# k'v of batches 1 to 7 as 64-column products, two heads side by side in the array

## The chip, the cores and the metric

The kernel runs on one core of one Trainium2 chip. A core has TensorE (the matrix array; the profile shows its products as PE and the loads of its weights as PEld), VectorE (DVE), ScalarE (ACT), GpSimd (POOL) and SyncE (SP), which issues most of the DMAs. The metric is device time in microseconds (us). Before the change it is 492.36 us, the median of three runs (492.21 to 492.42).

## The reference

Linear attention, and behind it a mixture of four experts over all tokens. There are 8 batches, 8 heads, 576 rows and 64 columns a head; 4608 tokens of 512 features; 4 experts with 1024 hidden units.

```python
def _attn_ref(q, k, v):
    phi = lambda x: np.where(x > 0, x, np.exp(x) - 1.0) + 1.0
    q_p, k_p = (phi(q), phi(k))
    kv = np.einsum('bhsd,bhse->bhde', k_p, v)
    z = np.sum(k_p, axis=2)
    num = np.einsum('bhsd,bhde->bhse', q_p, kv)
    den = np.einsum('bhsd,bhd->bhs', q_p, z)[..., None] + 1e-06
    return num / den

def _moe_ref(x, domain_probs, w1, w2):      # x: the attention's output, tokens by 512
    p = domain_probs / (domain_probs.sum(-1, keepdims=True) + 1e-09)
    for e in range(E):
        out += p[:, e:e + 1] * (np.maximum(x @ w1[e], 0.0) @ w2[e])
```

What the change touches is `kv` together with `z`: for each batch and head a matrix of 64 by 64, and the column sums of phi(k) as a 65th column. In the kernel v carries a constant column, so that both come from one product of k' (phi(k), 576 rows by 64) with v (576 rows by 65).

## The kernel before

**Staging.** A batch is one tile of 512 tokens (rows 0 to 511 of the batch, four to a partition) for the experts. The 64 rows that are left over of each batch are gathered into a ninth tile. The attention of batch b+1 is worked in between the expert products of tile b: while TensorE does the layers of tile j, the other engines load and prepare the next batch and TensorE does its small products at set places.

**Attention of a batch 1 to 7** (class `Batch`). `phi_act` (ACT, L343 and L346) and `phi_dve` (DVE, L351) make phi of k and q from the loaded data, the exponential passing through a PSUM bank of the pool "s"; `vcast` (ACT, L356) copies v to 16 bits. `left_act`, `left_v` and `left_dve` do the same for the 64 rows left over: `kl` holds their k' (with the other half of the partitions zero) and `vl` their v. `kv` makes the products of k' and v: for each pair of heads five products accumulate in PSUM, four over 128 rows each (L442) and one for the rows left over (L449). The stationary operand is k' of two heads, 128 columns, and the moving one v of two heads, 130 columns; so the result has four blocks of 64 by 65, of which the two on the diagonal are k'v of the two heads and the other two are not used. Two pairs go into one PSUM bank. Then ACT copies the diagonal blocks into `kvz` (L459), a tile whose other blocks stay zero, so that `nd` (L478) can multiply q' of two heads with it in one product of 130 columns and `norm` (L465, L466, DVE) can divide.

`kv` is called twice in a batch: `kv0` for pairs 0 and 1, `kv1` for pairs 2 and 3. Each call takes its own bank from the pool "s", which has two.

**Batch 0** (class `First`) is done before the experts start, with its rows laid out differently. Its `kv` (L612) already works by tiles: 64 rows and 64 columns of the array, the two halves on the array's diagonal.

**Experts.** For tile 0 the first layer of expert 0 (L661) and the second layer of all experts (L721) are plain products; all else goes by a Strassen-like scheme of seven products (`Block`, L873, for layer 1; `layer2_product`, L816, for layer 2), with its sums on POOL (`hidden_sum`, L783 to L789; `token_sum`, L854) and on DVE (L768 to L774 for the weights, L712 for the result, L857 for relu with an added part), and copies of banks on ACT (L884, L899, L906, L927).

**Order.** Nothing is left to a scheduler: each engine runs its instructions in the order in which the program issues them. All steps have a name and a due position (`CFG`, `put_at`) and are sorted by it; a step that is a generator stops at `yield` and goes on when its name comes again. The list `EARLY` writes out the order by hand for the first part, up to the first products of batch 3's turn; in it, a name that stands twice is the step's first part (for `kv` the products) and its second (the copies). In the later part a step's parts are issued directly one after the other. In a batch from 3 on, `kv0` is due at 17.5 and `kv1` at 19.1 of the batch's turn, with four products of layer 1, four of layer 2, four of layer 1 and four of layer 2 in between. In batch 1, two products of 512 columns stand between the two; in batch 2, two of 512 columns and eight of 256.

Of the kernel before, what the change touches and what calls it, by code (L numbers as in the profile page):

```python
# [11 lines left out]
FP32 = mybir.dt.float32  # L12
# [21 lines left out]
            lv=23.45,  # L34
            lk=15.35,
            lkd=16.3,
            kv=(33.6, 34.0),
            q=(36.4, 36.95, 40.2, 43.4),
            qd=(37.75, 39.0, 40.55, 44.7),
            lq=54.05,  # L40
# [13 lines left out]
            lv=10.36,  # L54
            lk=9.9,
            lkd=11.6,
            kv=(17.5, 19.1),
            q=(20.1, 22.1, 27.0, 30.0),
            qd=(21.75, 27.2, 30.2, 32.3),
            lq=33.9,  # L60
# [32 lines left out]
        "y0.33 k2 k0 y0.10 p1.020 p3.010 b1.k3 b1.lkm w211 p3.011 p1.021 y0.11 v3 s0.1 y0.20 w130 y0.12 y0.33 y0.13 p1.021 p2.021 p1.020 y0.21 y0.22 p2.020",  # L93
        "s2.0 s2.1 s2.3 b1.v1 p2.021 y0.13 p2.020 p6.020 p6.021 p6.020 t0.3 s2.2 y0.23 p6.021 b1.km3 p5.020 p7.020 b1.v2 q2 y0.23 s0.2 y1.10 t1.0 p7.020",
        "c22.020 b1.k1 p5.021 y1.11 p7.021 p7.021 w131 b1.km1 b1.k0 p4.020 p3.020 y1.20 y1.21 q0 b1.k2 p4.020 p4.021 c22.021 p3.020 b1.load5 p3.021 b1.km0",
        "y1.12 b1.v3 p4.021 b1.kv0 b1.km2 b1.load0 b1.kv0 y1.13 b1.kv1 b1.kv1 p3.021 y1.22 y1.23 b1.q3 y1.30 y1.13 y1.23 q1 y1.31 y1.32 y1.33 b1.q2 p1.031",
        "p1.031 y1.00 p1.030 p1.030 b1.qm3 y1.33 b1.qT3 b1.qm2 y1.01 b1.qT2 s3.0 s3.1 p2.030 y1.02 b1.qT3 b1.nd30 y1.03 s3.3 b1.qT2 b1.nd21 b1.loadlq p6.030",
        "b1.load2 lpr w220 p2.030 b1.nd30 w221 b1.q1 y1.03 p6.030 p5.030 b1.qm1 b1.nd31 p2.031 p7.030 b1.q0 b1.nd31 p6.031 b1.qm0 b1.next y2.00 p7.030 y2.01",
        "p4.030 p2.031 b1.qT1 p6.031 p4.030 b1.nd21 w230 b1.qT0 b1.nd20 p7.031 c22.030 p5.031 b1.qT0 b1.nd00 b1.xT3 s3.2 b1.nd20 b1.nd01 b1.qT1 p3.030 b1.xT2",
# [2 lines left out]
        "p1.100 p6.101 b1.qTl ts1.3 p3.031 b2.load0 y2.32 y2.33 b1.load3 t2.0 b2.lv p2.101 p6.100 p6.100 y2.33 b2.lkm y2.10 y2.11 t2.1 t0.1 b2.lq p2.100 p2.100",  # L102
        "y2.12 y2.13 b2.v0 p2.101 t3.0 b2.load5 p6.101 ts1.2 p7.100 y3.20 p7.100 b2.k3 y3.21 b2.v1 b2.load2 p5.100 p7.101 p7.101 b2.k1 b2.load3 y2.13 b1.nl",
        "y3.22 b2.km0 c22.100 b1.nl y3.23 b2.km3 y3.23 p3.100 p3.100 p4.100 b2.load9 p4.100 p5.101 b2.v2 b2.k2 b2.lqm y3.23 y3.10 y3.00 y3.01 p4.101 y3.02",
        "y3.03 p1.110 b2.km1 b2.kv0 p4.101 hs10.00 t1.1 b2.v3 y3.11 p1.110 p6.110 b2.kv0 c22.101 y3.03 b2.load4 b2.km2 p2.110 b2.kv1 p6.110 p2.110 y3.12 y3.13",
        "hs10.01 b2.q0 b2.kv1 p3.101 p7.110 t2.2 hs10.03 b2.load10 pr1 y3.30 p1.111 y3.31 b2.q1 p1.111 y3.32 t2.3 y3.33 y3.13 m10.21 p6.111 p5.110 hs10.02",
        "p3.101 b2.q3 b2.qm0 y3.03 b2.qm1 p7.110 p4.110 m10.20 y3.33 m10.21 hs10.10 t1.3 m10.51 b2.qm3 b2.q2 b2.load6 p2.111 m10.20 m10.50 hs10.11 m10.51",
        "p6.111 c22.110 b2.qm2 p4.110 b2.qTl p3.110 p3.110 m10.11 y3.13 m10.50 m10.11 p2.111 p7.111 p7.111 y3.33 b2.qT p1.120 m10.10 m10.61 p1.120 m10.10",
        "p2.120 p5.111 p2.120 m10.60 p6.120 m10.61 t0.2 t3.1 hs10.13 m10.31 m10.60 m10.30 c22.111 hs11.00 t1.2 p5.120 b2.load7 p4.111 b2.next m10.31 hs10.12",
# [13 lines left out]
def kernel(  # L123
# [10 lines left out]
    nc = tc.nc  # L134
# [6 lines left out]
    P = 128  # L141
    HP = P // 2
    CM = S // P
# [4 lines left out]
    NPAIR = H // 2  # L148
# [5 lines left out]
    DE = D + 1  # L154
# [54 lines left out]
    def aps(shape, dtype, name, more=""):  # L209
        return ppm.tile(shape, dtype, tag=CFG["BANK"].get(now[0] + more, "s"), bufs=2, name=name)  # L210
# [67 lines left out]
    class Batch:  # L278
# [153 lines left out]
                self.qT = pa.tile([P, CM, NPAIR, P], FP16, tag="qT", bufs=1, name="qT")  # L432
            (eng.copy if eng is nc.scalar else eng.tensor_copy)(out=self.qT[:, :, pair], in_=ps)

        def kv(self, pair0, n=2):
            ps = aps([P, 2, 2, DE], FP32, "psum_kv")
            for i in range(n):
                pair = pair0 + i
                hs = slice(2 * pair, 2 * pair + 2)
                a = pair % 2  # L440
                for c in range(CM):
                    nc.tensor.matmul(  # L442
                        out=ps[:, i],
                        lhsT=self.kp[:, c, hs],
                        rhs=self.vp[:, c, hs],
                        start=c == 0,
                        stop=False,
                    )
                nc.tensor.matmul(  # L449
                    out=ps[:, i],  # L450
                    lhsT=self.kl[:, pair],
                    rhs=self.vl[:, 2 * a : 2 * a + 2],
                    start=False,
                    stop=True,
                )
            yield
            for u in range(2):
                us = slice(u * HP, (u + 1) * HP)
                nc.scalar.copy(  # L459
                    out=self.kvz[us, pair0 : pair0 + n, u, :], in_=ps[us, 0:n, u, :]  # L460
                )

        def norm(self, dst, ps, n):
            recip = pa.tile([P, 4, 2, 1], FP32, tag="recip", bufs=3, name="recip")
# [470 lines left out]
    def order_of(at):  # L935

        return [x for _, x in sorted((at[n][i], (n, i)) for n in "vkq" for i in range(4))]

    def batch_steps(bt, nxt, put, at, at_next):

        mine = order_of(at)
        later = mine + (order_of(at_next) if nxt is not None else [])
        first = bt.b == 1

        def load(m):
            if m < len(later):
                (bt if m < len(mine) else nxt).load(*later[m])

        def load_left():
            if nxt is not None:  # L950
                nxt.alloc_left()
                nxt.load_left("k", "v", "q")

        b = bt.b

        def numerators(i0, n):
            yield from bt.nd(i0, n)
            for pair in range(NPAIR):
                if i0 < (pair + 1) * CM <= i0 + n:
                    yield  # L960
                    bt.dma_xT(pair)

        if not first:
            put(min(at["v"][0], at["k"][0], at["lv"], at["lk"]) - 0.01, f"b{b}.ones", bt.ones)
        for m, (n, i) in enumerate(mine):
            if n == "v":
                put(at[n][i], f"b{b}.v{i}", bt.vcast, i)
            else:
                put(at[n][i], f"b{b}.{n}{i}", bt.phi_act, n, i)
                put(at[n + "d"][i], f"b{b}.{n}m{i}", bt.phi_dve, n, i)  # L970
            if not first:
                put(at[n][i] + 1, f"b{b}.load{m}", load, m + NRAW)
        put(at["lv"], f"b{b}.lv", bt.left_v)
        for n in "kq":
            put(at["l" + n], f"b{b}.l{n}", bt.left_act, n)
            put(at["l" + n + "d"], f"b{b}.l{n}m", bt.left_dve, n)
        for i in range(2):
            put(at["kv"][i], f"b{b}.kv{i}", bt.kv, 2 * i)
        put(at["lqd"] + 1, f"b{b}.next", load_left)
        if not first:  # L980
            put(at["lqd"] + 2, f"b{b}.qTl", bt.dma_qTl)
        if first:
            put(at["qtl"], f"b{b}.qTl", bt.pe_qTl)
            for i in range(NPAIR):
                put(at["qt"][i], f"b{b}.qT{i}", bt.pe_qT, i, nc.scalar)
                for hf in range(2):
                    put(at["nd"][i], f"b{b}.nd{i}{hf}", bt.nd, i * CM + 2 * hf, 2)
                put(at["xt"][i], f"b{b}.xT{i}", bt.pe_xT, i)
            for i in range(NRAW):
                put(at["next"][i], f"b{b}.load{i}", load, len(mine) + i)  # L990
        else:
            put(at["qT"], f"b{b}.qT", bt.dma_qT)
            for i in range(6):
                put(at["nd"][i], f"b{b}.nd{i}", numerators, 3 * i, min(3, NPAIR * CM - 3 * i))
        put(at["nl"], f"b{b}.nl", bt.nd_left)
        if first:
            put(at["xl"], f"b{b}.xl", bt.pe_xl)
# [10 lines left out]
    b0, b1 = bts[0], bts[1]  # L1008
    on = {"A": nc.scalar, "V": nc.vector, "P": nc.gpsimd, "S": nc.sync}
    with tc.manual_schedule(  # L1010
# [7 lines left out]
        def put_at(pos, name, *g):  # L1018
            work.append((pos, len(work), name, g))
# [48 lines left out]
        for n, (j, e) in enumerate(units):  # L1068
            h, hss = [None, None], [[None] * 4, [None] * 4]
            at = base + 2 * NSLOT * n  # L1070
# [11 lines left out]
            if n == len(units) - 1:  # L1082
                order, at = (1, 2, 6, 5, 7, 3, 4), at + NSLOT
# [3 lines left out]
        for j in range(0, NTILES - 1):  # L1087
            at = base + 2 * NSLOT * E * (j - 1) if j else 0.0

            def put(pos, *g, at=at):  # L1090
                put_at(at + pos, *g)

            if j + 1 < B:
                nxt = bts[j + 2] if j + 2 < B else None
                batch_steps(bts[j + 1], nxt, put, ATTN[j > 0], ATTN[1])
            else:
                put(CFG["LATE"][0], "b0.alloc", b0.alloc_left)
                put(CFG["LATE"][0], "b0.load", b0.load_left, "q")
                put(CFG["LATE"][1], "b0.lq", b0.left_act, "q")
                put(CFG["LATE"][2], "b0.lqm", b0.left_dve, "q")  # L1100
                put(CFG["LATE"][2] + 1, "b0.qTl", b0.dma_qTl)
                put(CFG["LATE"][3], "b0.nl", b0.nd_left)
            for i in range(4):
                if j:
                    put(2 * NSLOT * E + CFG["TSUM"][i], f"ts{j + 1}.{i}", token_sum, j + 1, i)
                else:
                    put(base + CFG["TSUM1"][i], f"ts1.{i}", token_sum, 1, i)
# [48 lines left out]
```

## Time and profile before

| | |
|---|---|
| median of three runs | 492.36 us |
| profiled execution | 491.99 us |
| its span, first to last instruction | 490.2 us |
| granted TensorE clock over the span | 0.999 |
| TensorE products (PE) | 478.1 us busy, 4427 instructions |
| DVE, ACT, POOL | 382.4, 332.9, 358.8 us busy |
| k'v of batches 1 to 7 (L442, L449) | 140 products of 128 by 130, median 220 ns each |
| copies out of their banks (L459) | 28 on ACT, 64 by 130, median 263 ns each |
| k'v of batch 0 (L612) | 72 tiles of 64 by 65, median 191 ns each |

A product's time in the profile runs from its start to its modelled end, and products overlap in the array: a product that takes 220 ns alone is followed by the next after some 57 ns. So what a run of products costs is read from the starts, not from the durations. The page's second part cuts the span in 40 slices, and TensorE is at 90% or more in all but the first two and the last. The chain that ended last is followed back from the last instruction, at each step to what released it; its shares say where time could be taken away.

### The profile page before, as it was taken

What the parts mean: (1) busy time and instruction counts of PE and PEld (TensorE: products, weight loads), DVE (VectorE), ACT (ScalarE), POOL (GpSimd) and SP (SyncE); (2) the same over time, 40 slices, a digit from 0 to 9 for tenths busy, and PEclk for the clock granted to TensorE, in tenths of its full rate; (3) what the DMA queues carried; (4) which work ended last, traced back from release to release, by engine and by line L of the source; (5) the groups of instructions that cost most, each with busy time, mean ns of one, the idle gap of its engine ahead of it and who ended that gap; (6) DMA issues with size and microseconds to landing.
All of it is one profiled execution on the core that took longest, in us unless ns stands there. A gap on an engine that the chain in (4) does not pass through costs nothing.

```text
span 490.2 us, 11736 instructions
## 1 busy us (share of the span) xinstructions
PE 478.1 (98%) x4427; PEld 410.9 (84%) x4427; DVE 382.4 (78%) x801; ACT 332.9 (68%) x670; POOL 358.8 (73%) x341
## 2 busy tenths in 40 slices
PE   6899999999999999999999999999999999999996
PEld 2676766788898989898989898989898888888885
DVE  5768899998958896798769886978687756775686
ACT  5489979855896498749884889478954565446530
POOL 4655044688967896779776977697769877987775
PEclk9999999999999999999999999999999999999999
DMA  8999977642445245533453346323131020002003
GB/s 283 194 226 261 249 133 227 151 106 50 132 152 123 50 109 192 113 58 115 162 132 69 92 132 162 87 58 105 69 79 28 5 95 1 1 1 88 2 1 86
DMA packets 81016, 53.65 MB, mean 109 GB/s; under 512 B 45152, under 2 KB 73696, under 8 KB 80960
## 3 DMA queue, kind: packets, MB, share of 16 engines
q1 hardware_dynamic: 70512, 41.05, 31.4%
q0 software_dynamic: 9888, 11.41, 12.4%
q8 instruction: 34, 0.56, 0.5%
q10 hardware_dynamic: 560, 0.46, 0.3%
q14 instruction: 22, 0.18, 0.1%
HBM read 45.16 MB, written 9.44 MB: 111 GB/s over the span
## 4 chain that ended last, share of the span: by engine, by line
PE 91%; DVE 4%; ACT 1%; DMA 1%; issue 1%; SPq 1%; DVEq 0%; ACTq 0%
PE py L816 39%; PE pb L873 24%; PE pe L873 18%; PE py L721 4%; PE ph L661 1%; PE psum_nd L478 1%; DMA rawq<-in_q_dram 1%; PE psum_kv L442 1%; DVE acc L712 1%; PE pb L816 1%; SPq L546 0%; PE psum_nl L496 0%; PE pe L816 0%; DVE t L768 0%; DVE x_sb L638 0%
## 5 line engine op out<-in xcount | busy, mean ns | idle before, releaser
L712 DVE SCALAR_TENSOR_TENSOR acc<-py,p_sb,acc 128x256 f32<-128x256 f32 (+1 forms) x382 | 182.0, 489 | 45.6 <-PE py L816 40.5
L857 DVE CUSTOM_DVE_ANT_0 h<-pe,u 128x512 f16<-128x512 f32 x140 | 96.2, 688 | 44.4 <-PE pe L873 27.9
L873 PEld LDWEIGHTS <-w 128*128 128x128 f16 x1120 | 108.9, 98 | 17.6 <-issue 1.6
L783 POOL TENSOR_TENSOR hs<-h 128x512 f16<-128x512 f16 x64 | 74.0, 1156 | 57.9 <-DVE h L857 55.9
L816 PEld LDWEIGHTS <-h 128*128 128x128 f16 x1024 | 99.6, 98 | 12.0 <-issue 0.5
L816 PE MATMUL py<-w,h 128*128 128x256 f16 x744 | 106.4, 273 | 0.0
L884 ACT COPY u<-pb 128x512 f32<-128x512 f32 x140 | 82.6, 592 | 32.2 <-PE pb L873 29.4
L785 POOL TENSOR_TENSOR hs<-hs,h 128x512 f16<-128x512 f16 x64 | 75.1, 1174 | 25.6 <-PE py L816 23.2
L873 PEld LDWEIGHTS <-s 128*128 128x128 f16 x840 | 81.5, 98 | 11.4 <-issue 0.6
L873 PE MATMUL pb<-tt,w 128*128 128x256 f16 x560 | 83.7, 273 | 1.2 <-ACT u L884 1.2
L816 PEld LDWEIGHTS <-hs 128*128 128x128 f16 x768 | 74.4, 98 | 8.9 <-POOL hs L783 0.2
L789 POOL TENSOR_TENSOR hs<-h,hs 128x512 f16<-128x512 f16 x64 | 74.8, 1169 | 3.4 <-PE py L816 3.0
L787 POOL TENSOR_TENSOR h<-h 128x512 f16<-128x512 f16 x64 | 74.9, 1170 | 0.2
L816 PE MATMUL py<-t,hs 128*128 128x256 f16 x496 | 74.3, 273 | 0.0
L906 ACT ACTIVATE h<-pe 128x512 f16<-128x512 f32 x70 | 41.9, 599 | 44.0 <-PE pe L873 42.7
L899 ACT COPY pe<-pb 128x512 f32<-128x512 f32 x70 | 40.2, 576 | 39.3 <-PE pb L873 13.9
L927 ACT ACTIVATE h<-pb 128x512 f16<-128x512 f32 x70 | 42.0, 601 | 7.3 <-PE pb L873 7.2
L873 PE MATMUL pb<-tt,s 128*128 128x256 f16 x280 | 41.8, 272 | 0.1
L873 PE MATMUL pe<-tt,s 128*128 128x256 f16 x280 | 41.9, 273 | 0.0
L873 PE MATMUL pe<-xT,s 128*128 128x256 f16 x248 | 37.2, 273 | 0.0
L873 PE MATMUL pe<-xT,w 128*128 128x256 f16 x248 | 37.2, 273 | 0.0
L873 PE MATMUL pb<-xT,w 128*128 128x256 f16 x248 | 37.0, 273 | 0.0
(133 smaller groups left out, 607.8 us busy)
## 6 DMA issues: line engine op xcount, KB each, us to landing
out_dram<-acc SPq DMA_DIRECT2D x32, 256.0 KB, 2.5
w<-in_moe_w_dram POOLq DMA_DIRECT2D x14, 512.0 KB, 11.0
rawb<-in_k_dram SPq DMA_DIRECT2D x24, 256.0 KB, 3.1
rawb<-in_v_dram SPq DMA_DIRECT2D x24, 256.0 KB, 2.8
rawb<-in_q_dram SPq DMA_DIRECT2D x24, 256.0 KB, 2.7
rawq<-in_q_dram SPq DMA_DIRECT2D x4, 256.0 KB, 5.1
w<-in_moe_w_dram POOLq DMA_DIRECT2D x4, 256.0 KB, 6.4
rawb<-in_k_dram POOLq DMA_DIRECT2D x4, 256.0 KB, 8.6
```

The costliest lines, as they stand in the source:

```text
L712: nc.vector.scalar_tensor_tensor(out=acc, in0=ps, scalar=pscal, in1=acc, op0=AO.mult, op1=AO.add)
L783: nc.gpsimd.tensor_tensor(out=hs[0], in0=a21, in1=a22, op=AO.add)
L785: nc.gpsimd.tensor_tensor(out=hs[1], in0=hs[0], in1=a11, op=AO.subtract)
L787: nc.gpsimd.tensor_tensor(out=a21, in0=a11, in1=a21, op=AO.subtract)
L789: nc.gpsimd.tensor_tensor(out=hs[3], in0=a12, in1=hs[1], op=AO.subtract)
L816: nc.tensor.matmul(out=ps, lhsT=lhsT(k), rhs=rhs[:, k], start=first and k == 0, stop=k == FH - 1, skip_group_check=True,)
L857: nc.vector._custom_dve(TENSOR_ADD_SAT, out=out, in0=ps, in1=u, s0=BIG, s1=0.0)
L873: nc.tensor.matmul(out=ps[:, kk], lhsT=lk(kc), rhs=rhs[:, kc], start=first and kk == 0 and kc == 0, stop=kc == 1, skip_group_check=True,)
L884: nc.scalar.copy(u, self.b)
L899: nc.scalar.copy(self.e5, self.b)
L906: nc.scalar.activation(self.h[:, :, 0, 0:NH], self.e5, AF.Relu)
L927: nc.scalar.activation(self.h[:, :, 1, 0:NH], self.b, AF.Relu)
```

## The change

`kv` is called once per batch, where `kv1` stood. For each pair of heads and each of the five accumulation steps it issues two products, one per head: the stationary operand is k' of one head, 128 rows by 64 columns, the moving one v of that head, 65 columns. The first head's result goes to partitions 0 to 63 of the bank and uses columns 0 to 63 of the array; the second head's goes to partitions 64 to 127 and uses columns 64 to 127. No unused blocks are computed. All four pairs lie in one bank. Two copies per batch, each 64 by 4 x 65, take the place of four of 64 by 2 x 65.

On each engine this does the following. TensorE: 40 products and loads per batch instead of 20, in one run; the work between the two old runs moves ahead of it. ACT: the two copies that followed the first run are gone, the two that followed the second are twice as long. DVE, POOL and SP issue the same instructions in the same order. The steps `kv0` and `kv1` of `EARLY` for batches 1 and 2 become `kv` at the places of `kv1`.

```diff
@@ CFG
-            kv=(33.6, 34.0),
+            kv=34.0,
...
-            kv=(17.5, 19.1),
+            kv=19.1,
@@ EARLY
-        "y1.12 b1.v3 p4.021 b1.kv0 b1.km2 b1.load0 b1.kv0 y1.13 b1.kv1 b1.kv1 p3.021 ...
+        "y1.12 b1.v3 p4.021 b1.km2 b1.load0 y1.13 b1.kv b1.kv p3.021 ...
...
-        "y3.03 p1.110 b2.km1 b2.kv0 p4.101 hs10.00 t1.1 b2.v3 y3.11 p1.110 p6.110 b2.kv0 c22.101 y3.03 b2.load4 b2.km2 p2.110 b2.kv1 p6.110 p2.110 y3.12 y3.13",
-        "hs10.01 b2.q0 b2.kv1 p3.101 ...
+        "y3.03 p1.110 b2.km1 p4.101 hs10.00 t1.1 b2.v3 y3.11 p1.110 p6.110 c22.101 y3.03 b2.load4 b2.km2 p2.110 b2.kv p6.110 p2.110 y3.12 y3.13",
+        "hs10.01 b2.q0 b2.kv p3.101 ...
@@ class Batch
-        def kv(self, pair0, n=2):
-            ps = aps([P, 2, 2, DE], FP32, "psum_kv")
-            for i in range(n):
-                pair = pair0 + i
-                hs = slice(2 * pair, 2 * pair + 2)
+        def kv(self):
+            ps = aps([P, NPAIR, DE], FP32, "psum_kv")
+            for pair in range(NPAIR):
                 a = pair % 2
-                for c in range(CM):
-                    nc.tensor.matmul(
-                        out=ps[:, i],
-                        lhsT=self.kp[:, c, hs],
-                        rhs=self.vp[:, c, hs],
-                        start=c == 0,
-                        stop=False,
-                    )
-                nc.tensor.matmul(
-                    out=ps[:, i],
-                    lhsT=self.kl[:, pair],
-                    rhs=self.vl[:, 2 * a : 2 * a + 2],
-                    start=False,
-                    stop=True,
-                )
+                for c in range(CM + 1):
+                    for u in range(2):
+                        h = 2 * pair + u
+                        us = slice(u * HP, (u + 1) * HP)
+                        nc.tensor.matmul(
+                            out=ps[us, pair],
+                            lhsT=self.kp[:, c, h] if c < CM else self.kl[:, pair, us],
+                            rhs=self.vp[:, c, h] if c < CM else self.vl[:, 2 * a + u],
+                            start=c == 0,
+                            stop=c == CM,
+                            skip_group_check=True,
+                        )
             yield
             for u in range(2):
                 us = slice(u * HP, (u + 1) * HP)
-                nc.scalar.copy(
-                    out=self.kvz[us, pair0 : pair0 + n, u, :], in_=ps[us, 0:n, u, :]
-                )
+                nc.scalar.copy(out=self.kvz[us, :, u], in_=ps[us])
@@ batch_steps
-        for i in range(2):
-            put(at["kv"][i], f"b{b}.kv{i}", bt.kv, 2 * i)
+        put(at["kv"], f"b{b}.kv", bt.kv)
```

## The prediction

> **What bounds the kernel now.** I read the page's busy times first, then the chain that ended last, then that chain for the stretch from 100 to 470 us alone, then the timeline of TensorE around the products that change, and last the few waits of TensorE.
>
> ```profile
> PE 478.1 (98%) x4427; PEld 410.9 (84%) x4427; DVE 382.4 (78%) x801; ACT 332.9 (68%) x670; POOL 358.8 (73%) x341
> ...
> PE 91%; DVE 4%; ACT 1%; DMA 1%; issue 1%; SPq 1%; DVEq 0%; ACTq 0%
> ```
>
> TensorE is busy for 98% of the span and is 91% of the chain. The chain of the stretch from 100 to 470 us, by line:
>
> ```profile
> by line: PE py L816 48.4%; PE pb L873 27.5%; PE pe L873 20.7%; PE psum_nd L478 1.4%; PE psum_kv L442 1.2%; PE psum_nl L496 0.4%; PE psum_kv L449 0.3%; PE psum_xl L417 0.0%
> ```
>
> Not one piece of it lies on another engine: there, time taken from TensorE is time taken from the kernel, and k'v (L442, L449) is 1.5% of it. This holds for batches 3 to 7, whose k'v lies between 134 and 342 us. The timeline of TensorE around batch 3 (start, length, operation; a length is first start to last end, so that neighbours overlap):
>
> ```profile
> 134.09 0.60 PE L873 MATMUL pe<-xT,w 128*128 128x256 f16 x4
> 134.52 0.39 PE L442 MATMUL psum_kv<-vp,kp 128*128 128x130 f16 x4
> 134.75 0.22 PE L449 MATMUL psum_kv<-vl,kz 128*128 128x130 f16 x1
> 134.81 0.39 PE L442 MATMUL psum_kv<-vp,kp 128*128 128x130 f16 x4
> 135.03 0.22 PE L449 MATMUL psum_kv<-vl,kz 128*128 128x130 f16 x1
> 135.09 0.60 PE L873 MATMUL pb<-tt,w 128*128 128x256 f16 x4
> ...
> 136.84 0.39 PE L442 MATMUL psum_kv<-vp,kp 128*128 128x130 f16 x4
> ...
> 137.40 0.60 PE L873 MATMUL pe<-xT,s 128*128 128x256 f16 x4
> ```
>
> What counts is from start to start: 134.52 to 135.09 is 0.57 us for ten products of 128 by 130, 57 ns each; 136.84 to 137.40 the same. A batch pays 1.13 us, seven batches 7.9 us.
>
> The price of small tiles stands in batch 0, whose k'v already runs as pairs of tiles, 64 rows by 64 columns, on the array's diagonal (TensorE, 14.7 to 16.5 us):
>
> ```profile
> 14.71 0.28 PE L648 MATMUL psum_xh<-identh,x_sb 128*128 128x128 f16 x2
> 14.92 0.48 PE L612 MATMUL psum_kv<-vpos,kpos 64*64 64x65 f16 x18
> ...
> 15.91 0.48 PE L612 MATMUL psum_kv<-vpos,kpos 64*64 64x65 f16 x18
> 16.32 0.29 PE L648 MATMUL psum_xh<-identh,x_sb 128*128 128x128 f16 x2
> ```
>
> **The products.** Removed per batch: 20 products, 1.13 us. Added: 40 products of 64 columns by 65, alternating between the two halves of the array's columns.
> - Step. The 18 tiles of batch 0 last 0.48 us, of which a lone one is 0.19 (187 to 215 ns in the tile's view): 0.29 us for 17 steps, 17 ns each, 34 ns a pair. Bounds: at the low side 28 ns a pair, half of the 57 ns of 130 columns; at the high side the halves run one after the other, 30 ns each (57 ns at 130 columns and 109 ns at 256 put 65 columns at 30), so 60 ns a pair. I take 34: same columns, same moving length, same alternation; different are the rows, 128 in both halves instead of 64 each.
> - Body. 39 steps of 17 ns: 0.66 us.
> - Going in. The second transposition starts at 14.71 + 0.28 - 0.22 = 14.77 us and the tiles 0.15 us later, where 0.056 us is its usual step: 0.09 us lost.
> - Coming out. The last tile starts at 15.91 + 0.48 - 0.19 = 16.20, the next full product at 16.32: 0.12 us.
>
> Sum 0.66 + 0.09 + 0.12 = 0.87 us against 1.13: 0.26 us less per batch. The lower bound of the step gives 0.76 us (0.37 less), the upper 1.38 us (0.25 more). Two runs become one, so the switch is paid once; as two runs it would cost 1.08 us.
>
> [...]
>
> [...]
>
> **Place.** The first half's products move behind the work up to the second half's place. Inputs are no wait in batches 3 to 7: in batch 3 the last k' is finished by DVE at 133.90 us and the last copy of v by ACT at 133.22, and the new run starts near 136.3. What follows the removed half comes 0.57 us sooner: the product at 135.09 needs ACT's copy that ended at 133.70, that at 136.40 DVE's sum that ended at 135.28, that at 137.84 ACT's relu that ended at 136.45. With starts near 134.5, 135.8 and 137.6 all three hold. Priced at nothing; with the cover gone it is at most the 0.57 us of one half.
>
> **Copies and banks.** ACT loses four copies and gets two of 64 by 260:
>
> ```profile
> L459 ACT CAST kvz<-psum_kv x28: 255/263/282, 50.0 to 342.6; 64x130 f16<-64x130 f32 x28
> L623 ACT CAST kvz<-psum_kv x4: 208/208/211, 12.0 to 16.9; 64x65 f16<-64x65 f32 x4
> ```
>
> From 65 to 130 elements costs 55 ns, so 260 cost about 0.37 us: 0.75 us a batch instead of 1.05. ACT is off the path, no gain there. They start after all 40 products, which end earlier than the second half did, so q's activations behind them are not later. DVE, POOL and SP issue what they issued, DMAs too. One bank request fewer per batch in the pool "s" lets the next taker (q's exponential, on ACT behind the copies) in earlier: nothing.
>
> **Batches 1 and 2** lie where other engines set the pace (TensorE, 82 to 91 us, two windows):
>
> ```profile
> 82.39 0.59 PE L721 MATMUL py<-w,h 128*128 128x512 f16 x2
> 83.06 0.60 PE L873 MATMUL pb<-tt,s 128*128 128x256 f16 x4
> ```
>
> ```profile
> 89.28 0.60 PE L873 MATMUL pe<-tt,s 128*128 128x256 f16 x4
> 90.20 0.60 PE L873 MATMUL pb<-tt,w 128*128 128x256 f16 x4 [0.32 <-ACT u L884]
> ```
>
> Batch 2: two products of 512 columns step at 0.216 us, so TensorE was free at 82.82 and waited 0.24 us for ACT's copy of a bank (82.38 + 0.63). Without the half ahead of it, it waits 0.81. Then the merged run costs 0.30 more than the half it replaces, and the wait at 90.20 (four steps of 0.109 from 89.28 would be 89.72: 0.48 us, set by a chain through DVE and ACT from 82.0 on) swallows that. Between 0.26 less and 0.30 more; I take 0. Batch 1: the halves cost 0.61 and 0.57 us; the new run would start near 49.13, its third pair of heads near 49.48 needs k' that DVE ends at 49.36, its fourth near 49.65 the copy of v that ACT ends at 49.67. Between 0 and 0.31 less, after it a wait at 75.95 through DVE and ACT; I take 0.2.
>
> **Sum.** 5 x 0.26 + 0.2 + 0 = 1.5 us. The profiled execution took 491.99 us (span 490.2 and 1.8 around), 0.37 below the median of 492.36. 490.5 on the one, 490.8 on the other; I give 490.8. About 0.2%, 1 us, can be told from no change.
>
> **Rivals.**
> 1. Slower: the two halves of the columns do not run side by side when both use all 128 rows, because they share the rows' data. It decides from 47 ns a pair on ((1.13 - 0.21)/39 x 2). At 60 ns every batch costs 0.25 more: five batches 1.25, batch 1 0.2, batch 2 0.25 + 0.57 - 0.48 = 0.34 beyond the wait: 1.8 us, 494.1. For it: no row shows two tiles on the same rows. Against: batch 0 does as much per tile.
> 2. Far worse: each tile's load is exposed as well. Batch 0's loads come at 0.27 us per 17, 32 ns a pair; with 30 ns of product behind each, 40 x 62 ns + 0.21 = 2.7 us a batch, 1.6 more, about 503. Against: full-array loads hide behind products on the same rows.
> 3. No change: pairs step at 40 to 50 ns, or a bank or copy is late by what was gained. 491.4 to 493.3. Against: covers above of 0.4 us and more.
>
> **How the numbers follow.** Forecast 0.60 (own range 490.2 to 491.4, of which 0.02 is less than 0.2% away), rival 1 0.23, rival 2 0.05, rival 3 0.12. Faster 0.58, same 0.14, slower 0.28. The low end, 490.0, is the low bound of the step (5 x 0.37) with batch 1 in full and half of batch 2's bound (2.3 us); the high end, 494.8, holds rival 1 with 0.7 us for a batch-1 or batch-2 wait; rival 2 is left out.
>
> **What would show it.** In the profile after: from the first tile of batch 3's run to the next full product 0.78 us (0.66 and 0.12), and about 0.2 us between the last 256-column start and the first tile. Pairs at 60 ns: 1.3 us. TensorE rows behind the run start 0.26 us earlier per batch, 1.3 us in all at 342 us; the waits at 83.06 and 90.20 stay where they are. If the run is fast and the end is not earlier, a new wait of TensorE stands between 342 and 485 us. Wrong from the ground: a pair slower than 47 ns.

## The result and the profile after

The changed kernel takes 491.1 us (median of 18 runs, 489.7 to 492.7); the kernel before takes 492.35 us beside it (18 runs). The ratio is 0.9974, its 95% interval 0.9963 to 0.9985: 1.25 us faster, where 1.5 was forecast. The profiled execution took 491.24 us (before 491.99), its span is 489.5 us (490.2).

The page's busy times, its chain, and the row of its DMA queues that carries TensorE's instructions (packets, megabytes, share of the span of 16 DMA engines; before 34 packets):

```profile
PE 477.5 (98%) x4567; PEld 407.8 (83%) x4567; DVE 382.2 (78%) x801; ACT 330.8 (68%) x656; POOL 358.3 (73%) x341
...
q8 instruction: 35, 0.57, 0.5%
...
PE 91%; ACT 3%; DVE 2%; DMA 1%; issue 1%; SPq 0%; DVEq 0%; ACTq 0%
```

There are 140 products more (4567 for 4427) and 14 ACT instructions fewer; DVE and POOL are as before. TensorE is still busy 98% of the span. The chain from 100 to 470 us by line:

```profile
by line: PE py L809 48.5%; PE pb L866 27.5%; PE pe L866 20.9%; PE psum_nd L471 1.4%; PE psum_kv L443 1.0%; PE psum_nl L489 0.4%; ACT acc L703 0.1%; PE psum_xl L417 0.0%; issue 0.0%
```

k'v went from 1.5% of this stretch to 1.0%, and a piece of another engine has come in, ACT's L703 (before, L710). The run itself, on TensorE's timeline in batch 3 (start, length, operation; the columns are as in the prediction):

```profile
135.72 0.60 PE L809 MATMUL py<-w,hs 128*128 128x256 f16 x4
136.25 0.32 PE L443 MATMUL psum_kv<-vp,kp 128*64 128x65 f16 x8
136.40 0.20 PE L443 MATMUL psum_kv<-vl,kz 128*64 128x65 f16 x2
136.44 0.29 PE L443 MATMUL psum_kv<-vp,kp 128*64 128x65 f16 x8
136.56 0.20 PE L443 MATMUL psum_kv<-vl,kz 128*64 128x65 f16 x2
...
136.88 0.20 PE L443 MATMUL psum_kv<-vl,kz 128*64 128x65 f16 x2
137.01 0.61 PE L866 MATMUL pe<-xT,s 128*128 128x256 f16 x4
137.46 0.60 PE L866 MATMUL pb<-xT,w 128*128 128x256 f16 x4
```

Each pair of heads issues 8 tiles and then 2 for the rows left over, and the next pair starts 0.16 us after: 16 ns a tile, 32 ns a pair of tiles. From the last full product's start to the first tile it is 0.20 us where 0.109 is the usual step, from the last tile to the next full product 0.13. By the starts in the trace the run adds 0.863 us to the products around it (0.961 from the last full product to the next one, less 0.109 and with 0.011 lost in the step after). Before it was 2 x 0.567 = 1.134. The gain is 0.27 us in each of batches 3 to 7.

In batch 2 the two waits that the prediction followed (TensorE's timeline):

```profile
81.75 0.59 PE L714 MATMUL py<-w,h 128*128 128x512 f16 x2
83.00 0.60 PE L866 MATMUL pb<-tt,s 128*128 128x256 f16 x4 [0.65 <-ACT pe L892]
...
89.50 0.60 PE L866 MATMUL pe<-tt,s 128*128 128x256 f16 x4
90.12 0.60 PE L866 MATMUL pb<-tt,w 128*128 128x256 f16 x4
```

Two products of 512 columns end their turn at 81.75 + 0.43 = 82.18, so the first wait is 0.82 us, and the second 90.12 - 89.50 - 0.44 = 0.18. The stretch gives nothing, as forecast.

**A new wait.** TensorE and then ACT, 296 to 299 us:

```profile
297.16 0.60 PE L866 MATMUL pb<-xT,w 128*128 128x256 f16 x4
298.33 0.60 PE L809 MATMUL py<-w,h 128*128 128x256 f16 x4 [0.57 <-ACT acc L703]
```

```profile
296.07 0.60 ACT L877 COPY u<-pb 128x512 f32<-128x512 f32 x1
297.81 0.47 ACT L703 ACTIVATE acc<-py,p_sb 128x256 f32<-128x256 f32 x1 [1.13 <-PE pb L866]
```

From 297.16 the next start should come at 297.60; it comes at 298.33, 0.73 us late. It needs the bank that ACT's first addition into a new result tile `acc` (L703) reads, and that addition starts only at 297.81. The trace names a product as what ACT waits for, but that product had long been done. What ended at that time is a DMA: the store of the output block that lay in the same buffer, issued by SP at 293.19 and landed at 297.7. In the kernel before, the same store took 3.1 us and ACT wasn't late. The DMAs issued from 293 to 296 us (the last number is the median time to landing), after and then before:

```profile
q8 instruction: 1, 0.02, 1.9%
...
out_dram<-acc SPq DMA_DIRECT2D x2, 256.0 KB, 4.6
```

```profile
q8 instruction: 1, 0.02, 1.9%
...
out_dram<-acc SPq DMA_DIRECT2D x2, 256.0 KB, 3.2
```

**Where the time went.** The start of an execution differs by chance: the first q'k'v product of batch 0 stood at 12.83 us before and 13.09 after, and between 12.6 and 14.0 in the profiles that follow. So the profiles are compared from that product on. All kernels issue the same 3880 expert products in the same order; the table gives the starts of six of them (the 200th, 600th, 900th, 1600th, 2000th and 2400th) and the end of the last, against the kernel before (us, less than zero is earlier). Column "b1" is a product behind the k'v run of batch 1, "b2" one behind that of batch 2, and so on; "end" holds batch 7 too.

```
kernel                              b1     b2     b3     b4     b5     b6     end    wait at 247 / 298 (to 301)
changed                           -0.32  -0.34  -0.63  -0.91  -1.18  -0.73  -1.01   0    / 0.73
changed, again                    -0.29  -0.29  -0.56  -0.83  -0.77  -0.45  -0.72   0.34 / 0.60
fetch shifted by half a packet    -0.29  -0.28  -0.55  -0.82  -1.10  -1.37  -1.65   0    / 0
the same, again                   -0.32  -0.31  -0.59  -0.86  -1.13  -1.41  -1.69   0    / 0
fetch shifted by a whole packet   -0.28  -0.27  -0.54  -0.82  -0.91  -1.18  -1.46   0.19 / 0
batches 3 to 7 only               -0.12  -0.12  -0.41  -0.68  -0.96  -1.23  -1.51   0    / 0
the same, fetch shifted into it   -0.09   0.05  -0.24  -0.52  -0.76  -0.52  -0.80   0    / 0.51
batches 1 and 2 only              -0.32  -0.31  -0.32  -0.33  -0.33  -0.20  -0.20   0    / 0
tiles in two runs                 -0.20  -0.19  -0.26  -0.31  -0.35  -0.40  -0.45   0    / 0
five of a head in turn            -0.29  -0.29  -0.50  -0.72  -0.78  -0.41  -0.63   0.15 / 0.59
twenty of a head in turn           0.20   0.56   0.81   1.06   1.32   1.73   1.99   0    / 0.15
one run of full products          -0.14   0.89   0.88   0.96   0.96   0.96   0.96   0    / 0
```

About 0.1 us of every row is the kernel before, whose own batch 0 was that much slow in its profile.

### The profile page after: what moved, and what is told of

The parts are those of the page before. It is cut to its first block, busy times and chain, and to the rows that moved or that the text cites. A ratio compares the mean times of both kernels' runs of the same rounds, so it can differ in the third digit from the quotient of the medians.

```text
span 489.5 us, 12007 instructions
## 1 busy us (share of the span) xinstructions
PE 477.5 (98%) x4567; PEld 407.8 (83%) x4567; DVE 382.2 (78%) x801; ACT 330.8 (68%) x656; POOL 358.3 (73%) x341
## 4 chain that ended last, share of the span: by engine, by line
PE 91%; ACT 3%; DVE 2%; DMA 1%; issue 1%; SPq 0%; DVEq 0%; ACTq 0%
PE py L809 39%; PE pb L866 24%; PE pe L866 18%; PE py L714 4%; PE ph L654 1%; PE psum_nd L471 1%; DMA kraws<-in_k_dram 1%; PE psum_kv L443 1%; DVE acc L705 1%; PE pb L809 1%; PE pe L809 0%; DVE t L761 0%; PE psum_nl L489 0%; ACT kp L343 0%; ACT u L877 0%
```

## The experiments

**Which batches gain.** The new run in batches 3 to 7 alone, then in batches 1 and 2 alone (there the line reads `b <= 2`); `kv_all` is the changed kernel's `kv`, and the other batches keep the two runs of full products.

```diff
-        put(at["kv"], f"b{b}.kv", bt.kv)
+        if b >= 3:
+            put(at["kv"][1], f"b{b}.kv", bt.kv_all)
+        else:
+            for i in range(2):
+                put(at["kv"][i], f"b{b}.kv{i}", bt.kv, 2 * i)
```

> The new run in batches 3 to 7 only, batches 1 and 2 as before. Theory (TensorE sets the pace there and the run is 0.27 us shorter per batch): 5 x 0.27 = 1.35 us faster, about 491.0; from the last product before the run to the first after it 0.96 us in each of the five; the waits near 83.1 (0.24 us) and 90.2 us (0.49 us) as in the kernel before. Rival (the gain is spread over all seven batches): 5/7 of the 1.25 us measured, 0.9 us. Second rival (the loss in front of ACT's first addition near 298 us, seen in the changed kernel's profile, is caused by the change): it stands there again with about 0.7 us, and the time is about 0.7 us faster only.

> The new run in batches 1 and 2 only. Theory: batch 1 gives 0.2 us, batch 2 nothing: the wait near 83 us grows from 0.24 to 0.81 us, the one near 90.2 us shrinks from 0.49 to about 0.2; 492.15 us, no difference that can be told. From 95 us on everything starts 0.2 to 0.3 us earlier than before. Rival (every batch gives the same): 0.54 us, and the starts behind 95 us are 0.5 us earlier.

Batches 3 to 7: 490.95 us, ratio 0.9972 (0.996 to 0.9984). Batches 1 and 2: 492.07 us, ratio 0.9999 (0.9986 to 1.0013). The gain lies in batches 3 to 7, 0.27 us each. Batch 1 gives 0.2 (1.180 us before, 0.977 now, 0.09 of it a wait for v ahead of the fourth pair), batch 2 nothing. Surprising was that batches 3 to 7 alone are as fast as the whole change; this kernel has no wait at 298 us, and its stores of that stretch take 2.6 to 2.9 us.

**The tiles without the merging.** 64-column tiles, but in two runs, at the old places.

```diff
-        def kv(self):
-            ps = aps([P, NPAIR, DE], FP32, "psum_kv")
-            for pair in range(NPAIR):
+        def kv(self, pair0, n=2):
+            ps = aps([P, 2, DE], FP32, "psum_kv")
+            for i in range(n):
+                pair = pair0 + i
...
```

> The 64-column products, but in two runs per batch at the old places, two pairs and one bank each, four copies. Theory (each switch of the array's form costs 0.09 us in and 0.13 out): a run of 20 tiles costs 0.09 + 0.32 + 0.14 = 0.55 us against 0.57, so 0.03 a batch: 0.2 us faster in all, 492.2, not to be told from none. Rival (the gain is the tiles' own and the single run gives nothing): about 1.25 us faster.

492.33 us, ratio 1.0002 (0.9993 to 1.0012). TensorE in batch 3:

```profile
133.59 0.60 PE L867 MATMUL pe<-xT,w 128*128 128x256 f16 x4
134.12 0.32 PE L444 MATMUL psum_kv<-vp,kp 128*64 128x65 f16 x8
...
134.43 0.20 PE L444 MATMUL psum_kv<-vl,kz 128*64 128x65 f16 x2
134.56 0.61 PE L867 MATMUL pb<-tt,w 128*128 128x256 f16 x4
```

Going in and coming out cost the same as in the long run, about 0.2 us, but twice a batch: a run adds 0.545 us against 0.567 for the full products, so the tiles gain 0.04 us a batch. Merging is what makes them worth it.

**The merging without the tiles.** The full products of 130 columns in one run at the later place, two banks, in batch 2 the copies ahead of q's first activation.

```diff
+            banks = [aps([P, 2, 2, DE], FP32, "psum_kv") for _ in range(2)]
...
-                    for u in range(2):
+                    nc.tensor.matmul(
+                        out=ps[:, a],
+                        lhsT=self.kp[:, c, hs] if c < CM else self.kl[:, pair],
+                        rhs=self.vp[:, c, hs] if c < CM else self.vl[:, 2 * a : 2 * a + 2],
...
@@ EARLY
-        "hs10.01 b2.q0 b2.kv p3.101 ...
+        "hs10.01 b2.kv b2.q0 p3.101 ...
```

> The old products of 128 by 130, all four pairs in one run at the new place, in two banks, four copies (in batch 2 the copies stand ahead of the first activation of q on ACT, since both banks are taken). Theory: no gain; batches 3 to 7 cost 1.13 us as before, batch 2 waits 0.81 us near 83 us, its run costs 0.57 more behind that, and the wait near 90.2 us takes 0.49 of it: 0.1 us slower, 492.4, not to be told from none. Rival (the place of the run is what helps): about 1 us faster.

493.47 us, ratio 1.0025 (1.0016 to 1.0033): 1.2 us slower, which neither theory had. The runs add 1.13 us as expected, so the merging gives nothing by itself. The whole loss is one new wait of 1.04 us (TensorE), and by the table nothing else moves:

```profile
99.02 0.60 PE L865 MATMUL pb<-tt,w 128*128 128x256 f16 x4
100.49 1.03 PE L808 MATMUL py<-w,h 128*128 128x256 f16 x8 [0.88 <-DVE acc L704]
```

DVE's queue just before it has one long sum of weights. In this kernel and then in the changed one (DVE, and POOL at the same time):

```profile
96.84 1.64 DVE L762 TENSOR_TENSOR t<-w,t 128x1024 f16<-128x1024 f16 x1
```

```profile
96.78 1.15 POOL L777 TENSOR_TENSOR hs<-hs,h 128x512 f16<-128x512 f16 x1 [0.41 <-PE py L808]
```

```profile
96.47 0.68 DVE L763 TENSOR_TENSOR t<-w,t 128x1024 f16<-128x1024 f16 x1
```

```profile
96.47 1.70 POOL L778 TENSOR_TENSOR hs<-hs,h 128x512 f16<-128x512 f16 x1 [0.48 <-PE py L809]
```

The same operation of DVE takes 0.96 us more, while POOL runs a sum of its own from 96.78 to 97.93. In the changed kernel POOL runs that sum at the same time as DVE's too, and there POOL's is the longer one, 1.70 us instead of 1.15. That the two get in each other's way is argued from these two profiles and wasn't tried; that the 0.96 us reaches TensorE through the additions (L704) is shown by the chain of waits. It also shows how thin the cover is in batch 2's stretch.

**Do the halves run side by side?** For each pair of heads first the five tiles of one head, then the five of the other; and, further, all twenty of the first heads, then all twenty of the second.

```diff
-                for c in range(CM + 1):
-                    for u in range(2):
+                for u in range(2):
+                    for c in range(CM + 1):
```

```diff
-            for pair in range(NPAIR):
-                a = pair % 2
-                for c in range(CM + 1):
-                    for u in range(2):
+            for u in range(2):
+                for pair in range(NPAIR):
+                    a = pair % 2
+                    for c in range(CM + 1):
```

> The changed kernel with the five tiles of a pair's first head all issued before the five of its second, instead of alternating between the halves of the array. Theory (two tiles run side by side only where neighbours in the order lie in different halves): tiles step at 30 to 32 ns but for the one change of half, a run costs 40 x 31 ns + 0.2 = 1.4 us instead of 0.86, 0.3 us more per batch than the kernel before: 2 us slower than before, about 494.3. Rival (the array looks ahead and fills the other half whatever the order): steps of 16 ns, 491.1.

> The changed kernel with all 20 tiles of the first heads (one half of the array) issued before all 20 of the second heads. With five in turn the step went from 15.7 to 17.2 ns only, so the array takes tiles of the other half out of order or ahead. [...]

How far ahead of its turn a tile can start at the most, no run here measures.

Five in turn: 491.87 us, ratio 0.9999 (0.9982 to 1.0015); the body (first start to last) is 0.690 us against 0.629, so 17.7 ns a tile, and not the 30 ns that the theory of strict order wanted. The five tiles still overlap with the five of the other half. TensorE there:

```profile
135.79 0.34 PE L443 MATMUL psum_kv<-vp,kp 128*64 128x65 f16 x7
135.95 0.19 PE L443 MATMUL psum_kv<-vl,kz 128*64 128x65 f16 x1
```

The fifth tile of the first head, the one for the rows left over, is only the eighth to start: three tiles of the second head, issued after it, have started before it. Twenty in turn: 494.27 us in one execution; the body is 1.163 us, a run 1.40. TensorE there:

```profile
137.18 0.31 PE L443 MATMUL psum_kv<-vp,kp 128*64 128x65 f16 x4
137.33 0.20 PE L443 MATMUL psum_kv<-vl,kz 128*64 128x65 f16 x1
137.36 0.29 PE L443 MATMUL psum_kv<-vp,kp 128*64 128x65 f16 x4
...
137.68 0.29 PE L443 MATMUL psum_kv<-vp,kp 128*64 128x65 f16 x6
137.80 0.20 PE L443 MATMUL psum_kv<-vl,kz 128*64 128x65 f16 x1
137.81 0.23 PE L443 MATMUL psum_kv<-vp,kp 128*64 128x65 f16 x2
...
138.34 0.20 PE L443 MATMUL psum_kv<-vl,kz 128*64 128x65 f16 x1
138.47 0.50 PE L866 MATMUL pe<-xT,s 128*128 128x256 f16 x3
```

Five tiles take 0.16 us, 32 ns each, where one half works alone; around the change from the first half to the second (137.71 to 137.81) three pairs of tiles start 2 to 5 ns apart, and then it is 32 ns again. The first two starts that close together are the second and third with five in turn, the 17th and 18th with twenty: in both orders the second head's first tile (issued sixth, and 21st) starts three places ahead of its turn. So tiles on the same 128 rows do run side by side, and out of the order of issue, but in these two orders the other half's tile comes forward by only about three places. This run is rival 1 of the prediction made real: it gave 1.38 us for the run, measured is 1.40.

**A tile's price.** All forty products twice (the second time over the first, so the result is unaltered).

```diff
-            for pair in range(NPAIR):
+            for pair in (*range(NPAIR), *range(NPAIR)):
```

> The changed kernel with the 40 tiles of each batch issued twice in the same run, the second time starting the sums anew, so that the result stays. Theory (a tile costs 15.7 ns inside a run, the switch is paid once, and in batches 1 and 3 to 7 TensorE's time goes one to one into the kernel's): 0.63 us more in six batches, and in batch 2 0.63 less the 0.18 us that the wait near 90.1 us still holds: 4.2 us more than the changed kernel, 495.3. Rival (waits behind the run hide part of it): less than 3 us more.

496.19 us, ratio 1.009 (1.0066 to 1.0114), 4.3 us above the kernel before; its profiled execution took 5.4 us more than the changed kernel's. The body grows from 0.629 to 1.266 us, 16 ns a tile; seven times 0.638 is 4.5. In the profiles, from the first expert product to the end, it is 4.6 us more than the changed kernel, 0.17 of which is that its waits (0.43 us at 148 for ACT's addition, 0.47 at 210 for the DMA into `qT`) add up to more than that one's 0.73. Most of the rest is its batch 0, which ends 0.5 us later. The price of a tile is confirmed, on the path in all seven batches, batch 2 included.

**Is the store late because of TensorE's instructions?** The new theory: TensorE's instruction stream is fetched by DMA in packets of 16 KB (34 packets for the 8854 products and loads of the kernel before, 35 for the 9134 of the changed one). By the starts of the fetches there is one for every 255 products and loads (a line through all of them gives 254.7 before and 255.1 after; the expectations count 256), and one takes 0.88 to 1.67 us in these two profiles. A tile's turn has 976 products and loads before (3.83 packets) and 1016 after (3.98). So before the change the fetch drifts through the turns, and after it, it falls at nearly the same place in each (its phase): within the store of the third output block of tiles 1 to 4. The rival is that the store is late by chance or because the work around it stands closer. First the changed kernel unaltered, once more; then with 64 unused products of 2 columns in TensorE's warming run at the very start (128 instructions with their loads, half a packet); then batches 3 to 7 alone, which had no wait, with 40 of them (80 instructions), by which its fetch falls into the store.

```diff
+        for i in range(64 if now[0] == "warm0" else 0):
+            nc.tensor.matmul(
+                out=warm_ps[:, 0:2], lhsT=qz[:, 0, 0], rhs=qz[:, 0, 0, 0:2], start=True, stop=True
+            )
```

> The changed kernel once more, unaltered, beside the next two on one chip. In its first profile TensorE's instruction fetches (packets of 16 KB, 256 instructions) lie inside the stores of tiles 1 to 4 near 140.5, 191.4, 242.3 and 293.2 us, these take 3.1 to 4.5 us to land, and the last holds up ACT's next use of its buffer and TensorE by 0.73 us near 298. Theory (the place of the fetch is set by the count of instructions, which is the same in each execution): fetches lie there again and the stores take over 3 us again; 491.1. Rival (chance): stores of 2.3 to 2.9 us as in the profile with batches 3 to 7 alone.

> The changed kernel with 64 products of 2 columns (128 instructions, half a fetch) added to the warming products of the start, where TensorE waits for q anyway. Theory (fetches meet the stores by the count of instructions alone): fetches lie about 6 us away from the stores of tiles 1 to 4, these land in under 3.0 us, no wait of TensorE near 298, and the profiled execution is 0.4 to 0.7 us shorter than the changed kernel's: 490.5. Rival (fetches have nothing to do with it): stores of 3.1 to 4.5 us, 491.1 or, if the added products cost time, later.

> The new run in batches 3 to 7 only, with 40 products of 2 columns (80 instructions) added to the warming products, so that TensorE's instructions have the same numbers from batch 3 on as in the changed kernel. Theory (the count decides): fetches and stores coincide again, stores of tiles 1 to 4 over 3 us, and the wait near 298 may be back: 0.2 to 0.7 us slower than without the 40. Rival (it does not): stores of 2.6 to 2.9 us and 490.95 as without them.

The changed kernel again: 491.38 us, ratio 0.9975 (0.9963 to 0.9986), with the wait at two places this time (us in total, times, the longest):

```profile
PE py L809 <- ACT acc L703: 0.6, 2, 0.4
```

Shifted by half a packet: 490.41 us, ratio 0.9955 (0.9944 to 0.9967). The wait is gone (TensorE, 294 to 300 us), the fetches start 3.5 to 4.3 us ahead of the stores (6 were expected), and the store of that stretch takes 2.9 us:

```profile
297.15 0.60 PE L866 MATMUL pb<-xT,w 128*128 128x256 f16 x4
297.58 0.60 PE L809 MATMUL py<-w,h 128*128 128x256 f16 x4
```

```profile
out_dram<-acc SPq DMA_DIRECT2D x2, 256.0 KB, 2.9
```

Batches 3 to 7 alone, shifted into the store: 491.34 us, ratio 0.9977 (0.9968 to 0.9987); it has the wait that it didn't have:

```profile
297.43 0.60 PE L894 MATMUL pb<-xT,w 128*128 128x256 f16 x4
298.38 0.60 PE L837 MATMUL py<-w,h 128*128 128x256 f16 x4 [0.35 <-ACT acc L731]
```

By the table its path is 0.71 us longer than without the shift: 0.51 is this wait, and most of the rest is lost at a wait at 77 us for a DMA of weights, whose cause is not known. In whole times the two kernels can't be told apart (intervals 0.9968 to 0.9987 and 0.996 to 0.9984).

**Phase, or warming?** The added products also work TensorE longer at the start. So a whole packet of them, 128 products: the same phase again, and more warming; beside it half a packet once more.

```diff
-        for i in range(64 if now[0] == "warm0" else 0):
+        for i in range(128 if now[0] == "warm0" else 0):
```

> The changed kernel with 128 products of 2 columns added to the first warming run of TensorE, 256 instructions with their loads: one whole packet of the instruction stream, so the fetch comes back to the same phase in each tile's turn as in the changed kernel unaltered. It tells apart whether the shift by half a packet gained by the phase of the fetch or by the added warming itself. If by the phase: the stores of tiles 1 to 4 take 3.1 to 4.5 us again, a wait of TensorE of 0.3 to 0.9 us for ACT's addition stands at 247 or 298 us again, and the time is that of the changed kernel, 491.1 to 491.4 us (0.2 to 0.3% faster than before). If by the added warming: no such wait, and 490.4 us or less.

> The kernel with 64 added products of 2 columns (128 instructions, half a packet) once more, beside the one with a whole packet. By the phase of the fetch: 490.4 us, no wait at 247 or 298 us, stores of tiles 1 to 4 below 3 us, 0.7 to 1 us less than with the whole packet. If the gain was a chance of that call: the two come out alike.

A whole packet: 492.87 us, ratio 1.0011 (0.9997 to 1.0025). Half a packet: 490.66 us, ratio 0.9974 (0.9963 to 0.9985). The 2.2 us between them are more than the phase can be, and the time of the whole packet is not the 491.1 to 491.4 that was expected. The longer warming run now lasts until batch 0's first transposition (9.19 us, with no wait ahead of it; in the changed kernel it is at 8.49, behind a wait of 1.5 us), which the expectation had left out. And ten of the twelve runs had a granted clock of only 0.991 to 0.997 and took 491.56 to 495.16 us; the two at 0.999 or more, of which the profiled execution is one, took 491.33 and 491.36. The runs at 0.999 or more of the half packet have a median of 490.5 (7 of 12; in its first group 490.4, 5 of 6), those of the changed kernel beside that first group 491.3 (7 of 12). So at that clock the whole packet takes the changed kernel's time, by two runs, and the half packet some 0.8 us less; why the clock was lower in most runs of the whole packet isn't shown. More direct than whole times are the stores and waits. The times from issue to landing of the stores in question, with the fetch that stands nearest (start, us), from the trace:

```
kernel                             tile 1          tile 2          tile 3          tile 4
before                             2.41 (146.8)    2.45 (187.3)    2.82 (240.0)    3.12 (295.1)
changed                            3.14 (141.2)    3.28 (192.2)    3.69 (243.3)    4.51 (295.3)
changed, again                     3.12 (141.1)    3.36 (192.3)    4.12 (243.3)    4.38 (294.7)
batches 3 to 7 only                2.74 (144.6)    2.61 (195.5)    2.79 (247.2)    2.89 (288.5)
the same, fetch shifted into it    3.19 (141.5)    3.35 (192.6)    3.81 (243.6)    4.29 (294.6)
shifted by half a packet           2.60 (136.3)    2.82 (187.0)    2.85 (238.2)    2.71 (289.7)
the same, again                    2.68 (137.3)    2.57 (188.6)    2.77 (239.0)    2.69 (290.3)
shifted by a whole packet          3.29 (142.0)    3.34 (192.9)    3.97 (244.0)    2.84 (296.0)
```

The stores start at 140.4 to 141.4, 191.4 to 192.3, 242.3 to 243.2 and 293.2 to 294.4 us. Where the fetch starts 0.7 to 1.3 us behind the store, the store takes 3.1 to 4.4 us, the longer the later the fetch starts: 3.1 to 3.2 us at 0.67 to 0.79, 3.3 to 3.4 at 0.84 to 0.94, 3.7 to 4.1 at 0.97 to 1.03, 4.3 to 4.4 at 1.12 to 1.25. Where the fetch stands 3.2 us or more away, the store takes 2.4 to 2.9. A fetch two us behind it (296.0, 295.3) has done both. The whole packet brings the slow stores back, and TensorE is 0.19 us late at 247.5 again; half a packet takes them away. So the phase does it, and not the warming. From the table above, the path from batch 0's first q'k'v product is 0.64 to 0.68 us shorter in the half-packet kernels than in the changed one, and 0.93 to 0.97 shorter than in its second profile: its waits, 0.73 and 0.94. In whole times 18 runs of the half-packet kernel have a median of 490.6 and 30 runs of the changed one 491.3, 0.7 us less; the second group of runs alone, at a ratio equal to the changed kernel's, wouldn't show it: five of its twelve had a granted clock of 0.992 to 0.995 and a median of 491.7. By the profiles, the tiles in one run with the fetch moved away from the stores are the best of the versions, and their 490.4 us the lowest median; they beat the kernel before both times.

## Why the prediction was right, and where it was not

- **TensorE bounds the stretch from 100 to 470 us, so its time is the kernel's.** Right: twice the products cost 16 ns a tile in every batch, and the rows behind each run move by 0.27 us a batch, as the table has it.
- **Step 17 ns a tile, 34 a pair.** Measured 16 and 32. Batch 0's tiles were the right row to read it from, though they have 64 rows each and these 128.
- **Going in 0.09, coming out 0.12, the switch paid once.** Measured 0.093 and 0.129; 0.011 more is lost in the step behind. As two runs the tiles give almost nothing, as the 1.08 us said (by its own terms 1.07; measured 1.09).
- **Sum for a run 0.87 us, 0.26 less than before.** 0.863 and 0.27.
- **Batch 1: 0.2; batch 2: 0, its wait growing from 0.24 to 0.81 and the other shrinking by 0.30.** Right in each number: 0.20 with a short wait for v ahead of the fourth pair, and waits of 0.82 and 0.18.
- **Place of the moved half: nothing.** Right for the inputs. The cover is thinner than the text made it: with full products in one run a sum on DVE comes late and costs 1.04 us.
- **Copies off the path.** 372 ns each, 1.4 times the old copies' 263 for twice the columns; 0.74 us a batch against 1.05 (estimate 0.75), and TensorE has no wait for them.
- **The loads of the tiles.** The forecast gave them no time beside the step, and none shows: two loads fit into 32 ns a pair, and in the run of twenty in turn one half alone takes a new tile every 32 ns. The trace's records of these loads last 106 to 114 ns each and overlap one another, so a load's length is not its pace; in the kernel before, the loads of 128 columns lasted 95 to 99 ns at steps of 57. Here loads and products of tiles on the same 128 rows overlap.
- **Rivals.** Rival 1 falls for this order and is real for another: twenty of a head in turn cost 1.40 us a run. Rival 2 (0.06 us a tile) falls with the 16 ns. Rival 3's late bank is the nearest to what went wrong.
- **What was missed: "DVE, POOL and SP issue what they issued, DMAs too ... nothing".** One kind of DMA that no instruction of the kernel issues was left out: the fetch of TensorE's own instructions. With 40 more instructions a turn (3.98 packets where it was 3.83), its phase nearly stands still against the stores, and the store of an output block that ACT needs to be done meets it four times. This costs 0.73 us in one profile of the changed kernel, 0.94 in another. The sum of 1.5 us was right: without this wait the path is shorter by 1.65 us (0.1 of which is the kernel before's own slow batch 0), with it by 0.7 to 1.0. It also explains why batches 3 to 7 alone do as well: 0.2 us less gain, and no wait. The sign that the prediction named for such a case, a new wait of TensorE behind 342 us, was put too late; it stands at 247 and 298 us.

What stays open: why a fetch that starts later into a store holds it longer (it starts later from tile 1 to tile 4, and with it the stores get slower), on which DMA engine the two meet, and why the kernel with a whole packet of added products mostly ran at a lower granted clock.

## What to carry to other kernels

Here small products on both halves of the array's columns were worth their switch (some 0.2 us in and out) in one run of 40 (0.27 us a batch) and hardly in two runs of 20 (0.04), and only with products of the two halves alternating or a few places apart (twenty in turn cost 1.40 us a run, the full products 1.13); read step and switch from the starts of a run of that kind that the kernel already has. When TensorE's instruction count per turn changed here, from 976 to 1016, the fetch of its instructions moved against the stores: look at the buffers that wait for a DMA to land, above all for stores whose buffer is used again 3 to 4 us later. Compare profiles from a fixed product behind the start on, where a fifth of a percent is to be told apart, since the start alone differs by up to 1.4 us between the profiles here, and look at the granted clock of each run.

## What was not expected of the hardware

- An instruction fetch of 16 KB (all fetches together are 0.5% of the span of 16 DMA engines) lengthens a 256 KB store that it meets from 2.4 to 2.9 us to 3.1 to 4.5. There is one for every 255 of TensorE's products and loads, about 4 in a turn of 1016.
- Tiles of 128 rows by 64 columns start every 16 ns over the two halves, every 32 ns in one half alone, each with a load of its own. Five in turn on one half still overlap with the other half's (17.7 ns), and start out of the order of issue; twenty do so only for three pairs of tiles around the change.
- The same DVE sum of 128 by 1024 took 0.68 us in one kernel, where a sum of POOL that started at the same time took 1.70, and 1.64 in another, where that sum of POOL started 0.06 us ahead of it and took 1.15; the cause is not settled.
